# Fused beacon attention and squared-ReLU MLP: attention pairs released at 4.0 per MLP chunk instead of 4.4

## The chip, the cores and the metric

The kernel runs on one core of a Trainium2 chip. The core has a matrix engine (TensorE, PE in the profile, with its weight loads shown apart as PEld), a vector engine (VectorE, DVE), a scalar engine (ScalarE, ACT), a general engine (GpSimd, POOL), and SyncE (SP), which here only issues DMAs. Each engine runs its own instructions in order; the engines meet through semaphores. The metric is the device time of one execution in microseconds (us), lower being better.

## The reference

Inputs are `q`, `k`, `v` of shape 8 x 8 x 576 x 64 (batch, head, position, width), 16 "beacon" keys and values per batch and head, and the two MLP weights. Attention comes first, and its output, laid out as 4608 tokens of 512 numbers, is the input of the MLP:

```python
k_all = np.concatenate([beacon_k, k], axis=2)          # 16 + 576 keys
v_all = np.concatenate([beacon_v, v], axis=2)
scores = scale * np.matmul(q, k_all.transpose(0, 1, 3, 2))
scores = np.where(causal, -1000000000.0, scores)       # beacons are always seen
a = softmax(scores)
attn_out = np.matmul(a, v_all)
x = attn_out.transpose(0, 2, 1, 3).reshape(4608, 512)
h = x @ w_in                                           # 512 -> 2048
out = np.maximum(h, 0.0) ** 2 @ w_out                  # 2048 -> 512
```

All arrays are float32 outside the kernel; on the chip the matrix products take bfloat16 and accumulate in float32.

## The kernel before, in words

**Tiles.** Attention is worked in *pairs*: two heads of one batch. There are 4 pairs in a batch and 32 in all; pair `p` belongs to batch `p // 4`. For one pair the scores (L753, keys as weights, 64 rows per head, the two heads side by side) are cut into four pieces, each in two banks of PSUM, the accumulators of TensorE, which has eight banks. From batch 2 on the 16 pieces of a batch are placed in six groups, called strips here, of 3, 3, 3, 3, 2 and 2 pieces, and a strip goes under the gate of its first pair. ACT takes the exponential of a piece (L768) into a probability tile, DVE masks it (L783, L787), TensorE multiplies it by the values (L803, 30 matmuls a pair, with a column of ones for the sum), and DVE normalizes the result into `xn` (L818, L819).

**From attention to MLP.** For batch 0 TensorE transposes `xn`. For batches 1 to 7 SyncE issues five DMA transposes (L850), one for each tile of tokens, from `xn` into `xT`, once all four pairs of the batch are normalized. `xT` is a ring of 2304 tokens, four batches.

**The MLP** runs over nine chunks of 512 tokens. In the first half of a chunk (L931) each of 16 groups of four matmuls fills one PSUM bank, which ACT (L948) or DVE (L950) empties with the ReLU, and DVE squares two such results at once (L957). In the second half (L968) 64 matmuls accumulate four banks, ACT copies them out (L437), and SyncE stores them (L991). The second half uses a bank for 16 matmuls, the first one for four. Each matmul has a weight load of its own: a chunk has 64 on L931 and 64 on L968. Chunk 0 is split in two column ranges, and chunk 4 wraps around the ring, so that both have 128 shorter matmuls on L931. A chunk covers 512 tokens and a batch 576, so chunk `j` (1 to 7) reads `xT` of batch `j - 1` or before, and of batch `j` only the first tiles: four for chunks 1 and 2, three for chunks 3 and 4, two for 5 and 6, one for 7. Chunk 8 reads the rest of batch 7.

**Loads.** For batches 0 to 2 TensorE transposes queries and keys. For batches 3 to 7 SyncE loads them in float32 to staging buffers (L484, L483; eight buffers), POOL casts them to bfloat16 (L439), and SyncE issues two large DMA transposes per batch (L516), one for the queries and one for the keys. Batch buffers are double: batch `b` reuses those of `b - 2`.

**What sets the order.** A planner in the kernel (`Order.run`, L155) writes down the order of the instructions of each engine when the program is built, by playing the kernel through with modelled durations. Whenever an engine comes free there, it takes the operation of the lowest priority number whose inputs are modelled as ready, whose PSUM banks are free, and whose *gate* is open. On TensorE attention has lower numbers than the MLP, so without gates it would always come first. The gate of a pair (`gate`, L717) opens when the MLP work placed so far on TensorE (`progress`, in modelled us) reaches a value that grows with the pair's number; the first four pairs have none:

```python
return o.progress >= mlp_chunk_us * (LEAD + PACE * (p - HP))
```

`mlp_chunk_us` is 27.7, `LEAD` is -0.4, and `HP` is 4. An operation that would be ready but for its gate is kept as `fallback` (L237 to L246) and taken all the same if the engine has nothing else to do in the model. The chip then runs each engine's list in that order, waiting where something is later than the model had it.

Of the kernel before, what the change touches and what calls it, by code (L numbers as in the profile page):

```python
# [310 lines left out]
def kernel(  # L311
# [395 lines left out]
        return SPLIT if b < NSPLIT else WHOLE  # L707

    mlp_chunk_us = 27.7
    LEAD, PACE = -0.4, 0.225  # L710
    norm_ops = {}

    def add_pair(b, pr):
# [375 lines left out]
```

## Time and profile before

| | us |
|---|---|
| median of 3 runs | 343.65 (343.54 to 343.87) |
| profiled execution | 344.22 |
| its span, first to last instruction | 342.40 |
| TensorE busy | 325.1 |
| ACT busy | 195.0 |
| DVE busy | 160.3 |
| POOL busy | 81.1 |

The profile's page gives busy time by engine, the span in 40 slices, the DMA queues, the chain of work that ended last, and the costliest groups of instructions. Answers of the trace give more: what an engine waited for; the busy time in chosen stretches of the span, also of one line's instructions alone; and the instructions in order of time, where one row is a run of like instructions with its start, its length, what it writes and reads, its count (x) and, in brackets, the idle time before it with what ended that. `L753` is line 753 of the kernel. `SPq` is SyncE's queue, in which a DMA counts from when it is taken up to when it is issued, not to its landing. A group of words such as `kT<-qk_area` names the tile written and the one read.

### The profile page before, as it was taken

How to read it: one execution, taken by the hardware profiler on the slowest of the kernel's cores; microseconds unless marked ns; L12 is line 12 of the kernel's file. 1: busy time of each engine (PE TensorE's matmuls, PEld its weight loads, DVE VectorE, ACT ScalarE, POOL GpSimd, SP SyncE). 2: the span in 40 equal slices, each digit the busy share in tenths (PEclk: the TensorE clock that was granted, in tenths of full speed). 3: DMA queues.
4: the chain of work that ended last, by engine and by line, in shares of the span. 5: the costliest groups of instructions: out<-in, count | busy, mean ns of one | idle time of the engine just before them, and what ended most of it. 6: DMA issues, size and time to landing. Idle time of an engine off the chain costs nothing.

```text
span 342.4 us, 7074 instructions
## 1 busy us (share of the span) xinstructions
PE 325.1 (95%) x2838; PEld 175.7 (51%) x2876; DVE 160.3 (47%) x323; ACT 195.0 (57%) x301; POOL 81.1 (24%) x129
## 2 busy tenths in 40 slices
PE   2999999999999999999999799999999999999995
PEld 2677665454544544453557574444544444444442
DVE  6788978177425842385524483287403202301400
ACT  3987873588358564577554754597326326515611
POOL 6545802516124222423241126020000000000000
PEclk9999999999999999999999999999999999999999
DMA  9999999699979996999999889980041011011002
GB/s 166 197 205 221 206 204 208 134 252 204 188 164 215 197 199 145 255 188 224 133 209 220 184 177 207 219 170 24 15 117 63 0 61 63 0 61 63 0 29 93
DMA packets 139472, 50.33 MB, mean 147 GB/s; under 512 B 125808, under 2 KB 134512, under 8 KB 139440
## 3 DMA queue, kind: packets, MB, share of 16 engines
q1 hardware_dynamic: 129856, 40.91, 58.1%
q0 software_dynamic: 9376, 8.69, 15.5%
q8 instruction: 22, 0.36, 0.5%
q10 hardware_dynamic: 208, 0.29, 0.3%
q14 instruction: 10, 0.08, 0.1%
HBM read 37.22 MB, written 9.44 MB: 136 GB/s over the span
## 4 chain that ended last, share of the span: by engine, by line
PE 66%; DMA 19%; SPq 7%; DVE 4%; issue 2%; POOL 2%; ACT 1%; POOLq 0%; DVEq 0%; ACTq 0%
PE ps L931 28%; PE ps L968 26%; PE ps L803 5%; SPq L850 5%; PE ps L753 5%; DMA kT<-qk_area 5%; DMA stg<-in_k_dram 4%; DMA bks<-in_beacon_k_dram 3%; DMA stg<-in_v_dram 3%; DVE g L957 2%; DMA stg<-in_q_dram 1%; DMA qk_area<-in_q_dram 1%; SPq L484 1%; POOL w_in L892 1%; PE ps L635 1%
## 5 line engine op out<-in xcount | busy, mean ns | idle before, releaser
L931 PE MATMUL ps<-xT,w_in 128*128 128x512 bf16 (+3 forms) x688 | 134.3, 340 | 1.1 <-DMA xT<-xn 0.2
L968 PE MATMUL ps<-w_out,g 128*128 128x512 bf16 x554 | 127.9, 379 | 1.1 <-issue 0.2
L768 ACT ACTIVATE pt<-ps 128x832 bf16<-128x832 f32 (+4 forms) x128 | 102.9, 872 | 28.6 <-PE ps L753 28.5
L931 PEld LDWEIGHTS <-w_in 128*128 128x128 bf16 x704 | 64.9, 98 | 57.8 <-issue 7.7
L957 DVE TENSOR_TENSOR g<-g 128x1024 bf16<-128x1024 bf16 (+2 forms) x80 | 53.6, 673 | 76.9 <-ACT g L948 75.6
L948 ACT ACTIVATE g<-ps 128x512 bf16<-128x512 f32 (+2 forms) x117 | 66.3, 567 | 39.9 <-PE ps L931 39.2
L968 PEld LDWEIGHTS <-g 128*128 128x128 bf16 x576 | 54.1, 98 | 64.1 <-issue 2.9
L437 ACT COPY osb<-ps 128x512 f32<-128x512 f32 x36 | 21.3, 591 | 65.0 <-PE ps L968 60.4
L439 POOL CAST vb<-stg 128x512 bf16<-128x512 f32 (+1 forms) x36 | 24.3, 684 | 84.3 <-DMA stg<-in_v_dram 39.9
L439 POOL CAST qk_area<-stg 128x512 bf16<-128x512 f32 (+2 forms) x50 | 32.1, 645 | 50.6 <-DMA stg<-in_q_dram 33.8
L783 DVE TENSOR_TENSOR pt<-pt,tri 128x1024 bf16<-128x1024 bf16 (+1 forms) x36 | 23.9, 667 | 31.3 <-ACT pt L768 31.3
L803 PEld LDWEIGHTS <-pt 128*128 128x128 bf16 (+1 forms) x960 | 33.6, 98 | 7.6 <-issue 1.2
L950 DVE TENSOR_SCALAR g<-ps 128x512 bf16<-128x512 f32 (+2 forms) x43 | 25.7, 600 | 24.9 <-PE ps L931 24.5
L803 PE MATMUL ps<-vb,pt 128*128 128x65 bf16 (+1 forms) x960 | 34.9, 194 | 1.3 <-DVE pt L783 0.5
L753 PE MATMUL ps<-qT,kT 64*128 64x80 bf16 (+7 forms) x400 | 33.5, 282 | 2.6 <-DMA kT<-qk_area 2.1
L819 DVE TENSOR_TENSOR xn<-ps,rcp 128x640 bf16<-128x640 f32 (+2 forms) x36 | 27.0, 750 | 1.5 <-DVE rcp L818 0.2
L753 PEld LDWEIGHTS <-kT 64*128 64x128 bf16 x400 | 13.5, 96 | 23.2 <-issue 15.4
L818 DVE RECIPROCAL rcp<-ps 128x10 f32<-128x10 f32 (+2 forms) x36 | 7.5, 208 | 23.1 <-PE ps L803 23.0
L437 ACT COPY qT<-ps 128x576 bf16<-128x576 bf16 x12 | 7.5, 640 | 6.4 <-PE ps L635 5.0
L439 DVE COPY kT<-ps 128x576 bf16<-128x576 bf16 x12 | 8.9, 751 | 2.8 <-PE ps L638 1.9
L787 DVE TENSOR_TENSOR pt<-pt,tri 80x160 bf16<-80x160 bf16 x32 | 10.0, 312 | 0.0
L635 PE MATMUL ps<-ident,sparek 96*128 96x96 bf16 x18 | 1.5, 229 | 6.0 <-DVE sparek L439 6.0
(49 smaller groups left out, 71.7 us busy)
## 6 DMA issues: line engine op xcount, KB each, us to landing
out_dram<-osb SPq DMA_DIRECT2D x17, 512.0 KB, 3.3
stg<-in_v_dram SPq DMA_DIRECT2D x21, 256.0 KB, 5.0
stg<-in_q_dram SPq DMA_DIRECT2D x20, 256.0 KB, 4.7
stg<-in_k_dram SPq DMA_DIRECT2D x15, 256.0 KB, 5.1
w_in<-in_moe_w_in_dram POOLq DMA_DIRECT2D x4, 512.0 KB, 8.2
w_out<-in_moe_w_out_dram POOLq DMA_DIRECT2D x4, 512.0 KB, 10.9
stg<-in_v_dram SPq DMA_DIRECT2D x7, 224.0 KB, 4.2
qk_area<-in_k_dram POOLq DMA_DIRECT2D x4, 288.0 KB, 12.7
```

Of the source, the lines that this page charges most:

```text
L437: nc.scalar.copy(dst, src)
L439: eng[e].tensor_copy(dst, src)
L753: nc.tensor.matmul(st[:, hj, col:col + t1 - t0], kT[x.b % 2][hp, x.pr, 128 * c:128 * c + 128], qT[x.b % 2][hp, x.pr, t0:t1], start=True, s ...
L768: nc.scalar.activation(pt[x.take_pt.held[0]][:, :, off:off + width], pair(box["qk"], k)[:, :, 0:width], AF.Exp, bias=0.0, scale=scale)
L783: nc.vector.tensor_tensor(out=d, in0=d, in1=tri[:, m0:m0 + m, :][:, None].to_broadcast([128, 2, m, 128]), op=ALU.min)
L803: nc.tensor.matmul(a[:, hj, (t - tl[0]) * (D + 1):(t - tl[0] + 1) * (D + 1)], P[0:rr, hj, o:o + 128], vb[b % 2][0:rr, c, h, :], start=(c = ...
L819: nc.vector.tensor_tensor(out=xn[b % 2].rearrange("p t (h d) -> p h t d", d=D)[:, 2 * pr:2 * pr + 2, tl[0]:tl[0] + nt], in0=a[:, :, :, 0:D ...
L931: nc.tensor.matmul(h[:, lo - spans[0][0]:hi - spans[0][0]], w_in_sb[:, mc, ft * 128:(ft + 1) * 128], xT[:, mc, lo % RING:lo % RING + hi - lo],
L948: nc.scalar.activation(dst, h, AF.Relu, bias=0.0, scale=1.0)
L950: nc.vector.tensor_scalar(out=dst, in0=h, scalar1=0.0, scalar2=None, op0=ALU.max)
L957: nc.vector.tensor_tensor(out=d, in0=d, in1=d, op=ALU.mult)
L968: nc.tensor.matmul(o, G[:, fc, ts * 128:(ts + 1) * 128], w_out_sb[:, fc, :], start=(fc == 0), stop=(fc == NFT - 1))
```

## The change

`PACE` goes from 0.225 to 0.25. The gates of the 28 gated pairs (4 to 31) run from -0.4 to 5.675 chunks before and from -0.4 to 6.35 after: the last pair is released 0.675 chunk later, and the first at the same place. The last pair of batch `b` is released at `b - 0.65` chunks after the change; before it was at `0.9 b - 0.625`. Nothing else in the kernel is edited; the planner's order follows from the gates.

```diff
     mlp_chunk_us = 27.7
-    LEAD, PACE = -0.4, 0.225
+    LEAD, PACE = -0.4, 0.25
     norm_ops = {}
```

## The prediction

> **What bounds the kernel now.** I read the page's engine rows and clock first, then the list of what TensorE waited for, then the busy time by stretch, and last the order of TensorE and of the SyncE queue around the waits.
>
> ```profile
> PE 325.1 (95%) x2838; PEld 175.7 (51%) x2876; DVE 160.3 (47%) x323; ACT 195.0 (57%) x301; POOL 81.1 (24%) x129
> ...
> PEclk9999999999999999999999999999999999999999
> ```
>
> ```profile
> PE ps L635 <- DVE sparek L439: 6.0, 1, 6.0
> PE ps L753 <- DMA kT<-qk_area: 2.1, 1, 2.1
> PE ps L803 <- DVE xn L819: 0.5, 1, 0.5
> ```
>
> The columns of the second list are us in total, times, longest. TensorE (PE) is the bound: busy 95% of the 342.4 us at full granted clock. Its largest wait, 6.0 us, is the start, before anything that the change touches. The next is one wait of 2.1 us for the transposed keys.
>
> ```profile
> 92.12:253.38 161.26, 157.36 (x1435) 84.32 (x1456) 77.58 (x135) 96.10 (x140) 40.95 (x63) 1.00 0.90 172
> 156.07:190.31 34.24, 32.01 (x305) 18.44 (x308) 14.41 (x26) 20.41 (x30) 10.35 (x16) 1.00 1.12 197
> 253.38:282.75 29.37, 29.21 (x134) 13.32 (x136) 5.53 (x8) 11.89 (x20) 0.00 (x0) 1.00 0.14 54
> ```
>
> A row gives the stretch, its length, busy PE, PEld, DVE, ACT, POOL, the clock and the DMA share. 92.12 to 253.38 holds the attention of batches 3 to 7; TensorE idles there for 161.26 − 157.36 = 3.90 us, 2.23 of it in batch 5's stretch (second row). The third row is MLP alone: 136 weight loads in 29.37 us, 0.216 us each, so a chunk of 128 loads is 27.65 us. ACT (96.10 of 161.26 us) and DVE (77.58) have room. So whatever the order, TensorE's work is the same, and an edit to the order can win at most some part of those 3.90 us.
>
> **Does the gate set the order now?** A pair's scores may be placed once the MLP work already placed reaches the gate. I count that work in chunks, by weight loads of the two MLP lines, cut at the first score strip of batches 3 to 7 and at the last of batches 3, 4, 5 and 7. L931 first, then L968:
>
> ```profile
> 0.00:92.12 92.12, 16.82 (x192) 1.00 1.07 199
> 92.12:113.77 21.65, 1.79 (x20) 1.00 0.92 198
> 113.77:123.84 10.07, 3.77 (x40) 1.00 1.19 200
> 123.84:149.26 25.42, 2.03 (x24) 1.00 0.96 198
> 149.26:156.07 6.81, 2.20 (x24) 1.00 1.14 167
> 156.07:176.99 20.92, 1.79 (x20) 1.00 1.13 185
> 176.99:190.31 13.32, 5.41 (x56) 1.00 1.10 216
> 190.31:220.71 30.40, 7.04 (x76) 1.00 0.99 193
> 220.71:239.06 18.35, 5.32 (x60) 1.00 0.52 112
> ```
>
> ```profile
> 0.00:92.12 92.12, 7.18 (x80) 1.00 1.07 199
> 92.12:113.77 21.65, 4.38 (x48) 1.00 0.92 198
> 123.84:149.26 25.42, 5.97 (x64) 1.00 0.96 198
> 156.07:176.99 20.92, 4.30 (x48) 1.00 1.13 185
> 176.99:190.31 13.32, 1.48 (x16) 1.00 1.10 216
> 190.31:220.71 30.40, 5.89 (x64) 1.00 0.99 193
> ```
>
> Chunks 0 and 4 are split in two column ranges, so their 128 L931 loads count as 64: 64 off the first row, 28 off the x56, 36 off the x76. The sum at 92.12 us is 192 − 64 + 80 = 208, or 1.625 chunks; then 2.156, 2.469, 3.156, 3.344, 3.875, 4.219, 5.031, 5.500. The gates of the first pairs of batches 3 to 7 (pairs 12, 16, 20, 24, 28) are 27.7·(−0.4 + 0.225·(p − 4)) us, in chunks 1.40, 2.30, 3.20, 4.10, 5.00, and the strips came at 1.625, 2.469, 3.344, 4.219, 5.031: behind the gate by 0.23, 0.17, 0.14, 0.12 and 0.03. So batches 3 to 6 started when their keys and queries were expected, and only batch 7 at its gate. After the change the gates are 1.60, 2.60, 3.60, 4.60, 5.60. Batch 3's start stays (1.625 is past 1.60), as does all before it; the orders part about 100 us in, where its third pair's gate rises from 1.85 to 2.10 and that strip now stands at about 2.03. From batch 4 on the gate comes after the data by 0.13, 0.26, 0.38 and 0.57 chunk, and it sets the start.
>
> **Step 1, the wait for the keys goes: −2.07 us.**
>
> ```profile
> 190.32 0.76 PE L753 MATMUL ps<-qT,kT 64*128 64x496 bf16 x8 [2.07 <-DMA kT<-qk_area]
> ```
>
> This is batch 6's first strip: TensorE stood from 188.25 to 190.32 us until the transposed keys landed. With the gate at 4.60 in place of the present 4.219, 0.381·128 = 49 more weight loads stand ahead of it, 49·0.216 = 10.5 us, so TensorE comes there at about 198.8 us at the earliest, 8.5 us after the landing. If that cover is gone (loads later by more than 8.5 us), the wait is back at up to its present size. What releases those keys does not get later by the change: their loads and casts reuse buffers of batch 4, whose last strip moves from 3.156 to about 3.35, some 5 us on from 149 us, and the loads come well behind that. On SyncE's queue the five transposes of attention output (xT) move behind loads that now follow them; loads gain by that, unless an xT stands in the queue before its normalization is done, in which case the loads behind it wait as well, and the 8.5 us have to carry it. What is late next is nothing on TensorE's list: the largest other wait past 92 us is the 0.5 above.
>
> **Step 2, the MLP's input comes later: 0 us, hidden by about 4 us or more.** All pairs of a batch come later, so its normalized output, and the SyncE transposes that make the MLP's input, too. Chunk j reads only the first tiles of batch j: three for chunks 3 and 4, two for chunk 5, one for chunk 7.
>
> ```profile
> 111.43 4.90 SPq L516 DMA_TRANSPOSE qT<-qk_area  x1
> 116.43 3.60 SPq L516 DMA_TRANSPOSE kT<-qk_area  x1
> 120.08 2.52 SPq L484 DMA_DIRECT2D stg<-in_v_dram  x3
> 122.69 6.75 SPq L850 DMA_TRANSPOSE xT<-xn  x5
> 159.49 7.50 SPq L850 DMA_TRANSPOSE xT<-xn  x5
> 189.80 6.72 SPq L850 DMA_TRANSPOSE xT<-xn  x5
> 246.27 6.42 SPq L850 DMA_TRANSPOSE xT<-xn  x5
> ```
>
> ```profile
> DMA to landing us min/median/max: 2.3/2.5/5.7
> ```
>
> ```profile
> 143.23 2.84 PE L931 MATMUL ps<-xT,w_in 128*128 128x512 bf16 x12
> 179.34 1.04 PE L931 MATMUL ps<-xT,w_in 128*128 128x256 bf16 x8
> 217.12 1.03 PE L931 MATMUL ps<-xT,w_in 128*128 128x512 bf16 x4
> 282.98 7.31 PE L931 MATMUL ps<-xT,w_in 128*128 128x512 bf16 x33
> ```
>
> The needed tile of chunk 3 lands at 122.69 + 2·1.35 + 2.5 = 127.9 us, 15.3 us ahead of its first matmul at 143.23. For chunk 4 it is 159.49 + 2·1.50 + 2.5 = 165.0 against 179.34, 14.3 us; for chunk 5, 193.6 against 217.12, 23.5 us; for chunk 7, 248.8 against 282.98, 34.2 us. The last pair of batch b is released at b − 0.65 after the change. The second strips of pairs 15 and 19 now stand 0.08 and 0.18 behind their gates (2.156 against 2.075, 3.156 against 2.975). With 0.08, the shifts are 2.43 − 2.156, 3.43 − 3.156, 4.43 − 3.875 and 6.43 − 5.500 chunks, or 7.6, 7.6, 15.3 and 25.7 us; what stays is 7.7, 6.7, 8.2 and 8.5 us. With 0.18 it is 2.8 less everywhere, at the least 3.9, at chunk 4. I cost it at 0. If the cover goes, each us of lateness beyond it is a us of TensorE, as none of its other work is free to fill it.
>
> **Step 3, small waits in the new order: 0 us, between −1.0 and +2.5.** Of the 3.90 us of idle time, 1.67 lies outside batch 5's stretch: once TensorE waited 0.5 us for DVE in an attention-times-values step (the xn row). MLP alone leaves 29.37 − 29.21 = 0.16 us in 29, or 0.7 in the other 127 us, so the most that the small waits can give is −1.0. The other way, one wait of 0.5 in each of five batches is 2.5 us. Pairs 30 and 31 (gates 6.10 and 6.35) move into chunk 6, where ACT is busy for 11.89 of 29.37 us, so their exponentials find room. The order after 100 us is new, so I take the same number as now, 0 net: the row at hand is one in five batches.
>
> Strips, matmuls, exponentials and DMAs are the same in number, and the last 60 us are MLP alone in both, so steps 1 to 3 are the sum: −2.07 + 0 + 0. The profiled execution took 344.22 us (342.4 span, 1.8 around it), 0.57 above the median of 343.65; after it, 342.15 with a span of 340.3, and the median 343.65 − 2.07 = 341.6 us. The low end is 343.65 − 2.07 − 1.0 = 340.6; the likeliest case's own range ends at 341.6 + 3·0.5 = 343.1, three new small waits.
>
> **The rivals.**
>
> *The wait moves (no change), 0.14.* The supply of batches 4 to 6 was late against the gate throughout, the DMA share in batch 5's stretch is 1.12, and an order that leaves SyncE in another state can have one strip stand ahead of its keys again. Against it: from batch 4 on the gate lies 3.6 to 16 us of MLP work past the present starts. One wait of the same size gives 343.65. That the change does not do what it says belongs here: a gated strip is still placed when TensorE would stand idle in the written order. Pair 23's first strip, for one, stands at 159.54 us, right after batch 5's first and far ahead of its gate of 3.875:
>
> ```profile
> 159.54 0.58 PE L753 MATMUL ps<-qT,kT 64*128 64x496 bf16 x4
> ```
>
> If that took most of them, the time would stay at 343.65.
>
> *The MLP's input is late (slower), 0.17.* At batch 3 the query and key transposes (4.90 + 3.60) and three loads (2.52) stood directly ahead of the xT transposes, 11.1 us of SyncE's queue. If after the change they come between the normalization and the xT of batch 4, chunk 4's input is 11.1 − 6.7 = 4.4 us late, and the time is 341.6 + 4.4 = 346.0 us. It decides from 6.7 + 2.07 = 8.8 us of such lateness. Against it: the xT moves later, away from the transposes of keys, which end at 120.0 us while batch 3's xT would come at about 130.
>
> [...] After the 6.05 us at the start, the first transposes ran slower than the same ones later (per row of six):
>
> ```profile
> 6.05 0.66 PE L635 MATMUL ps<-ident,sparek 96*128 96x96 bf16 x6 [6.05 <-DVE sparek L439]
> 55.28 0.42 PE L635 MATMUL ps<-ident,sparek 96*128 96x96 bf16 x6
> ```
>
> The clock row reads 9 there all the same. [...]
>
> *Many small waits, 0.05.* After the change the last strips of every batch fall in the first half of a chunk, in which every matmul group needs a bank emptied by ACT or DVE; now only batches 3 and 4 have that pattern, with one wait of 0.5 between them. At two waits of 0.5 in each of five batches, 5.0 us, the time is 341.6 + 5.0 = 346.6; it decides from five.
>
> **How the numbers follow.** The forecast, 341.6 us, has 0.64. A measurement here can tell about 0.2%, 0.7 us, from no change. Of the 0.64, 0.61 is faster by more than that and 0.03 within it; of "the wait moves", 0.03 is faster, 0.09 the same and 0.02 slower; the two slower rivals add 0.22 less 0.01. So faster 0.64, same 0.13, slower 0.23. The range goes from 340.6 to 344.5, into the slower rivals' milder forms.
>
> **What would show it.** Step 1: no wait for kT on TensorE past 92 us, and first strips of batches 4 to 7 at 2.6, 3.6, 4.6 and 5.6 chunks. Step 2: no wait of L931 for xT past 92 us, with 4 us or more between landing and first use. Step 3: TensorE's idle time from 92 us to the start of chunk 6 near 1.8 us. It would be wrong if L931 waits at the heads of chunks 3 to 7, or if L753 waits for another batch's keys.

## The result and the profile after

The changed kernel takes 341.27 us (median of 20 runs) against 343.68 us for the kernel before (20 runs); the ratio is 0.9946, with a 95% interval of 0.9923 to 0.9969. The ratio is estimated from the executions that were not in a slower state, and is not the quotient of the two medians, which is 0.9930. The forecast was 341.6 us. The profiled execution took 341.50 us with a span of 339.80.

The page's engine row of the changed kernel, and the list of all that TensorE waited for from 93 us to 340 us (us in total, times, longest):

```profile
PE 324.1 (95%) x2838; PEld 175.5 (52%) x2876; DVE 161.4 (47%) x324; ACT 194.5 (57%) x300; POOL 82.3 (24%) x129
```

```profile
PE ps L968 <- issue: 0.6, 4, 0.2
```

The 2.1 us for the keys (L753 <- kT) are gone, and so is the 0.5 us for DVE. What is left is four times 0.16 us.

The stretches of the changed kernel between the first score strips of batches 3, 4, 5, 6 and 7, all engines (columns as in the prediction), and after them a stretch of the same length as the prediction's 161.26 us:

```profile
92.93:128.34 35.41, 35.14 (x292) 17.27 (x296) 16.80 (x29) 20.92 (x31) 11.81 (x18) 1.00 1.03 200
128.34:163.74 35.40, 35.02 (x292) 17.29 (x296) 17.31 (x29) 21.02 (x31) 11.43 (x17) 1.00 1.10 200
163.74:199.32 35.58, 35.31 (x358) 23.54 (x360) 17.84 (x28) 21.62 (x32) 12.65 (x18) 1.00 0.96 200
199.32:234.73 35.41, 35.03 (x292) 17.27 (x296) 16.24 (x29) 21.12 (x31) 6.90 (x11) 1.00 0.78 145
...
92.93:254.19 161.26, 159.71 (x1393) 84.88 (x1414) 73.95 (x126) 96.59 (x143) 42.80 (x63) 1.00 0.88 174
```

Every batch now takes 35.4 to 35.6 us, with 0.27 to 0.38 us of idle time. Over 161.26 us TensorE idles for 1.55 us in place of 3.90.

The weight loads of the MLP in the same stretches, L931 first, then L968:

```profile
0.00:92.93 92.93, 16.79 (x192) 1.00 1.09 199
92.93:128.34 35.41, 5.88 (x64) 1.00 1.03 200
128.34:163.74 35.40, 5.88 (x64) 1.00 1.10 200
163.74:199.32 35.58, 12.13 (x128) 1.00 0.96 200
199.32:234.73 35.41, 5.88 (x64) 1.00 0.78 145
```

```profile
0.00:92.93 92.93, 7.19 (x80) 1.00 1.09 199
92.93:128.34 35.41, 5.87 (x64) 1.00 1.03 200
128.34:163.74 35.40, 5.88 (x64) 1.00 1.10 200
163.74:199.32 35.58, 5.89 (x64) 1.00 0.96 200
199.32:234.73 35.41, 5.86 (x64) 1.00 0.78 145
```

With chunk 4's 128 counted as 64, the stretches hold 128 loads each: exactly one chunk between first strips, which come at 1.625, 2.625, 3.625, 4.625 and 5.625 chunks. From batch 4 on that is 0.025 past the gate, so the gate sets the start.

The gain lies in the part from batch 3's first strip to the last matmul: 246.32 us before (92.12 to 338.44) and 242.96 after (92.93 to 335.89), 3.36 us less. The start before it has the same order in both and was 0.81 us longer in this execution of the changed kernel. Over all profiled executions with batch 3's first strip at 1.625 chunks, that strip came between 92.1 and 94.6 us, so the start varies by more than 2 us whatever the kernel (the last section says where). Below, "the late part" is the time from batch 3's first strip to the end of the last matmul, which leaves that variation out.

### The profile page after: what moved, and what is told of

Its sections match the earlier page's. It is cut to its first block, busy times and chain, and to the rows that moved or that the text cites. A ratio compares the mean times of both kernels' runs of the same rounds, so it can differ in the third digit from the quotient of the medians.

```text
span 339.8 us, 7073 instructions
## 1 busy us (share of the span) xinstructions
PE 324.1 (95%) x2838; PEld 175.5 (52%) x2876; DVE 161.4 (47%) x324; ACT 194.5 (57%) x300; POOL 82.3 (24%) x129
## 4 chain that ended last, share of the span: by engine, by line
PE 86%; DMA 6%; DVE 3%; issue 2%; ACT 1%; POOL 1%; SPq 0%; DVEq 0%; ACTq 0%; POOLq 0%
PE ps L968 36%; PE ps L931 34%; PE ps L803 8%; PE ps L753 7%; DMA bks<-in_beacon_k_dram 3%; DMA qk_area<-in_q_dram 1%; DMA stg<-in_v_dram 1%; DVE qk_area L439 1%; DVE g L957 1%; PE ps L635 1%; POOL w_in L892 0%; DVE g L950 0%; DVE pt L783 0%; ACT qT L437 0%; ACT pt L768 0%
## 5 line engine op out<-in xcount | busy, mean ns | idle before, releaser
L931 PE MATMUL ps<-xT,w_in 128*128 128x512 bf16 (+3 forms) x689 | 134.1, 340 | 1.5 <-DMA w_in<-in_moe_w_in_dram 0.7
L968 PE MATMUL ps<-w_out,g 128*128 128x512 bf16 x553 | 128.3, 379 | 1.5 <-issue 0.6
L768 ACT ACTIVATE pt<-ps 128x832 bf16<-128x832 f32 (+4 forms) x128 | 102.9, 873 | 24.5 <-PE ps L753 24.3
L931 PEld LDWEIGHTS <-w_in 128*128 128x128 bf16 x704 | 64.9, 98 | 56.3 <-issue 4.9
L968 PEld LDWEIGHTS <-g 128*128 128x128 bf16 x576 | 53.8, 98 | 64.6 <-issue 4.6
L957 DVE TENSOR_TENSOR g<-g 128x1024 bf16<-128x1024 bf16 (+2 forms) x80 | 52.3, 658 | 67.7 <-ACT g L948 67.1
L439 POOL CAST vb<-stg 128x512 bf16<-128x512 f32 (+1 forms) x36 | 25.2, 708 | 75.6 <-DMA stg<-in_v_dram 61.3
L803 PEld LDWEIGHTS <-pt 128*128 128x128 bf16 (+1 forms) x960 | 33.7, 97 | 6.6 <-DVE pt L783 0.5
L803 PE MATMUL ps<-vb,pt 128*128 128x65 bf16 (+1 forms) x960 | 35.1, 194 | 0.3 <-ACT pt L768 0.2
L753 PE MATMUL ps<-qT,kT 64*128 64x80 bf16 (+7 forms) x400 | 33.6, 282 | 0.4 <-ACT pt L768 0.4
L753 PEld LDWEIGHTS <-kT 64*128 64x128 bf16 x400 | 13.6, 96 | 21.9 <-issue 17.3
```

The costliest lines, as they stand in the source:

```text
L439: eng[e].tensor_copy(dst, src)
L753: nc.tensor.matmul(st[:, hj, col:col + t1 - t0], kT[x.b % 2][hp, x.pr, 128 * c:128 * c + 128], qT[x.b % 2][hp, x.pr, t0:t1], start=True, s ...
L768: nc.scalar.activation(pt[x.take_pt.held[0]][:, :, off:off + width], pair(box["qk"], k)[:, :, 0:width], AF.Exp, bias=0.0, scale=scale)
L803: nc.tensor.matmul(a[:, hj, (t - tl[0]) * (D + 1):(t - tl[0] + 1) * (D + 1)], P[0:rr, hj, o:o + 128], vb[b % 2][0:rr, c, h, :], start=(c = ...
L931: nc.tensor.matmul(h[:, lo - spans[0][0]:hi - spans[0][0]], w_in_sb[:, mc, ft * 128:(ft + 1) * 128], xT[:, mc, lo % RING:lo % RING + hi - lo],
L957: nc.vector.tensor_tensor(out=d, in0=d, in1=d, op=ALU.mult)
```

## The experiments

All times are medians, and ratios are to the kernel before, measured beside the experiment.

**1. Only the wait taken away.** The order of every engine stays that of the kernel before.

```diff
-                    st = pair(box["qk"], k)
+                    st, kept = pair(box["qk"], k), (x.b + (group[0][0].p == 24 and group[0][1] == 0)) % 2
...
-                                kT[x.b % 2][hp, x.pr, 128 * c:128 * c + 128],
-                                qT[x.b % 2][hp, x.pr, t0:t1],
+                                kT[kept][hp, x.pr, 128 * c:128 * c + 128],
+                                qT[kept][hp, x.pr, t0:t1],
```

> Every engine keeps the order of the kernel before; only the first score strip of batch 6 reads the keys and queries of batch 5, which lie ready, in place of its own (that strip's scores are therefore another batch's). Theory A (the gain is the wait of batch 6's first strip for its keys): the wait of 2.07 us at L753 goes and nothing takes its place, 343.7 - 2.1 = 341.6 us, ratio about 0.994. Rival B (the gain is the even spacing of the strips, and the wait alone would be paid later): the time stays within 0.7 us of 343.7, since the strips stand as close as before.

Measured: 343.01 us, ratio 0.9967 (0.9939 to 0.9995); late part 245.09 us, 1.23 less than before. TensorE's order of time around three places (start, length, what, count, and in brackets the wait):

```profile
189.93 0.76 PE L753 MATMUL ps<-qT,kT 64*128 64x496 bf16 x8
...
201.19 0.66 PE L803 MATMUL ps<-vb,pt 80*128 80x65 bf16 x16 [1.04 <-POOL vb L439]
...
221.94 0.76 PE L753 MATMUL ps<-qT,kT 64*128 64x496 bf16 x8 [0.35 <-DMA kT<-qk_area]
```

The first strip of batch 6 runs without a wait, but 1.39 us come back further on: TensorE, now earlier, meets batch 6's values before POOL has cast them, and batch 7's keys before they land. The interval of the ratio reaches from theory A's 0.994 almost to 1, so the run times do not decide between A and B; the trace does. Of the 1.23 us, 0.47 is the wait for DVE (L803 for `xn`, at 112.8 us in the kernel before), which is absent here although the order there is the same. So taking the 2.07 us away won some 0.8 us and not 2.07, and what is missing came back as new waits: theory A was too simple. The wait is real, and it is the first of several that all say the same: in batches 6 and 7 the supply on the chip runs behind the written order. I call this theory A2: the change gains because it puts *all* of those uses behind the supply.

**2. Half of the change.** `PACE` 0.2375.

```diff
-    LEAD, PACE = -0.4, 0.225
+    LEAD, PACE = -0.4, 0.2375
```

> PACE 0.2375, half of the change. Batch 6's first strip is placed at 4.37 chunks in place of 4.21, 0.16*27.65 = 4.4 us later, more than the wait of 2.07 us. Theory A: no wait for the keys of batch 6, and nearly the whole gain, 341.6 us. Rival B: half of the spread gives about half of the gain, 342.6 us, or less.

Measured: 341.46 us, ratio 0.9931 (0.9907 to 0.9956); late part 243.17 us; no wait over 0.2 us after 92 us. Half of the spread has the whole gain, against rival B.

**3. Batch 6 alone later.**

```diff
-            return o.progress >= mlp_chunk_us * (LEAD + PACE * (p - HP))
+            return o.progress >= mlp_chunk_us * (LEAD + (0.25 if b == 6 else PACE) * (p - HP))
```

> The kernel before, with the gates of batch 6's four pairs alone at PACE 0.25: its first strip moves from 4.21 to 4.62 chunks, the order is the same up to there, and batch 7's strips are pressed together with those of batch 6 (the last one at 5.81). Theory A: the wait goes and the time is 341.6 us. Rival B: the strips stand closer together than in either kernel, so small waits take the gain away, 343 to 344 us.

Measured: 342.66 us, ratio 0.9964 (0.9940 to 0.9988); late part 244.75 us, 1.57 less than before. What TensorE waited for after 92 us:

```profile
PE ps L753 <- DMA kT<-qk_area: 1.1, 1, 1.1
PE ps L968 <- issue: 0.3, 2, 0.2
PE ps L803 <- DVE xn L819: 0.2, 1, 0.2
```

The wait for keys is now batch 7's (at 220.7 us), whose first strip was moved from 5.03 to 5.21 chunks only. Neither number was met: about half of the gain, and most of what is missing is again the supply (1.1 us) and not closer strips.

**4. The lead without the pace.** Every gate 0.2 chunk later at the old pace.

```diff
-    LEAD, PACE = -0.4, 0.225
+    LEAD, PACE = -0.2, 0.225
```

> PACE 0.225 as before, but LEAD -0.2 in place of -0.4: every gate 0.2 chunk later, batch 6's first strip at 4.34 chunks (0.13*27.65 = 3.6 us later than before) and batch 7's at 5.21. Theory A2: no wait for batch 6's keys, most of the gain, 341.6 us, without any change of pace. Rival B: within 0.7 us of the time before, 343.5 us.

Measured: 341.27 us, ratio 0.9949 (0.9929 to 0.9970); late part 243.21 us; no wait at all listed after 93 us. The gain is had with pairs at 4.4 per chunk.

**5. The pace without the lead.** The new pace, with every gate 0.4 chunk earlier.

```diff
-    LEAD, PACE = -0.4, 0.225
+    LEAD, PACE = -0.8, 0.25
```

> PACE 0.25 as after the change, but LEAD -0.8 in place of -0.4: every gate 0.4 chunk earlier, so that batches 3 to 6 are placed where they stand in the kernel before (batch 6's first strip at 4.21), and batch 7 at 5.21. Theory A2: the wait for batch 6's keys is back, 1 to 2 us, and the time is 343 to 343.7 us although pairs are released at four per chunk. Rival B (the pace, the even spacing, brings the gain): 341.5 us.

Measured: 343.14 us, ratio 0.9996 (0.9963 to 1.0030); late part 245.50 us, 0.82 less than before. Batch 6's first strip in TensorE's order of time:

```profile
189.81 0.76 PE L753 MATMUL ps<-qT,kT 64*128 64x496 bf16 x8 [2.00 <-DMA kT<-qk_area]
```

The wait is back at its old size, and the gain in run time is gone although pairs are released at four per chunk. Of the 0.82 us in the late part, 0.47 is the wait for DVE that does not show here, and 0.07 the keys'. Experiments 4 and 5 together settle it: the pace by itself is worth nothing that the run time shows, and some 0.3 us in the late part; where the strips of batches 6 and 7 stand against their supply is what counts.

**6. No late supply at all.** Batches 6 and 7 read the buffers of the batch before, with the matmul lines of experiment 1.

```diff
+                    st, kept = pair(box["qk"], k), (x.b + (x.b >= 6)) % 2
...
-                            vb[b % 2][0:rr, c, h, :],
+                            vb[(b + (b >= 6)) % 2][0:rr, c, h, :],
```

> The order of the kernel before on every engine, but batches 6 and 7 read the keys, queries and values of the batch before them, which lie ready (their attention is therefore of the wrong batch). With the first strip alone on old keys, 1.39 us of new waits came: values of batch 6 (1.04), keys of batch 7 (0.35). Theory A2 (the chip's supply runs behind the written order in batches 6 and 7, and the change's gain is the cover against that): no wait on kT or vb past 180 us, 341.6 us, a ratio near 0.994, and near 244.2 us from batch 3's first strip to the last matmul (246.3 before, 243.0 after the change). Rival B2 (the even order itself saves more than 1 us): about 342.5 us or more, near 245 us in that part.

Measured: 354.65 us, ratio 1.0344 (1.0307 to 1.0381). TensorE's waits after 92 us:

```profile
PE ps L803 <- POOL vb L439: 3.0, 1, 3.0
PE ps L753 <- DMA kT<-qk_area: 2.8, 1, 2.8
```

The edit did not do what it was meant to: waits on values and keys grew instead of going. The last key transpose on SyncE's queue, and batch 6's last strip on TensorE, show why:

```profile
212.47 2.97 SPq L516 DMA_TRANSPOSE kT<-qk_area  x1
```

```profile
219.11 1.16 PE L753 MATMUL ps<-qT,kT 64*128 64x464 bf16 x10 [2.81 <-DMA kT<-qk_area]
```

That transpose is batch 7's, and it landed 6.60 us after its issue, at 219.07. It fills the buffer that batch 6 now reads, and in the written order it stands ahead of this strip, so the strip waited for batch 7's keys. In the same way the wait of 3.01 us ended with a cast of batch 7's values. On top came the clock, which fell to 0.50 after each of the two waits (last section). So the late uses of batch 6 were tied to a later supply, and the run tells nothing on A2.

**7. The change taken twice.** `PACE` 0.275.

```diff
-    LEAD, PACE = -0.4, 0.225
+    LEAD, PACE = -0.4, 0.275
```

> PACE 0.275, the change taken twice. Last strips of batches 3, 6 and 7 are placed at 2.75, 5.93 and 6.80 chunks (after the change 2.44, 5.43 and 6.43). With the change the MLP input of chunks 3, 6 and 7 lands 5.1, 10.0 and 6.3 us ahead of its first use; 8.6, 13.8 and 10.2 us later it would be late by 3.5, 3.8 and 3.9 us, so the theory that each us of lateness past the cover is a us of TensorE gives 341.3 + 11 = 352 us, with waits of L931 for xT of this size. Rival: batch 7 and batch 3 are filled with other work in the written order, and the time stays under 345 us.

Measured: 354.79 us, ratio 1.0325 (1.0286 to 1.0364). The two largest entries of TensorE's waits after 92 us:

```profile
PE ps L753 <- ACT pt L768: 4.4, 6, 1.3
PE ps L931 <- DMA xT<-xn: 2.6, 2, 1.8
```

That the time is near the expectation is luck, as its make-up is another: the waits for xT are smaller than 11 us, and a larger part stands at the strips. At the heads of chunks 3 and 6 the written order has strips placed one after the other, some ahead of their gates (at chunk 3 both strips of batch 4's last pair, whose gate is at 3.725), as nothing else was ready there in the model; on the chip most of them wait for ACT's exponentials to empty their banks. Read so, the late MLP input is paid there more than at L931. On top came the clock. Stretches around the first of these places, and two rows of TensorE's order of time in it:

```profile
139.80:143.60 3.80, 1.19 (x14) 0.58 (x14) 0.18 (x1) 3.80 (x7) 1.84 (x3) 1.00 0.77 157
143.60:150.40 6.80, 5.83 (x47) 3.18 (x45) 2.56 (x7) 2.76 (x4) 0.00 (x0) 0.50 0.71 168
```

```profile
145.04 1.86 PE L931 MATMUL ps<-xT,w_in 128*128 128x512 bf16 x4 [0.75 <-DMA xT<-xn]
146.70 1.86 PE L803 MATMUL ps<-vb,pt 128*128 128x65 bf16 x30
```

The same step in the changed kernel:

```profile
143.52 1.08 PE L803 MATMUL ps<-vb,pt 128*128 128x65 bf16 x30
```

After 3.8 us in which TensorE was busy for 1.19 us only, the granted clock is 0.50 for 6.8 us. Four MLP matmuls take 1.86 us where they took 1.03 us, and the 30 matmuls on the values 1.86 us where they took 1.08. All waits listed after 92 us come to 8.2 us; the 10.2 us at a granted 0.50 (a second place has 3.4) cost some 4.5 us by estimate, at the 0.83 us that the four matmuls lose in 1.86. Together that is 12.7 of the 13.5 us by which this kernel is slower than the changed one.

**8. The new pace, later still.** `LEAD` -0.2 at `PACE` 0.25.

```diff
-    LEAD, PACE = -0.4, 0.225
+    LEAD, PACE = -0.2, 0.25
```

> PACE 0.25 with LEAD -0.2: every gate 0.2 chunk later than after the change, the last strips of batches 3 to 7 at 2.62, 3.56, 4.62, 5.56 and 6.62 chunks against 2.44, 3.43, 4.43, 5.43 and 6.43, so 3.6 to 5.2 us later. After the change the MLP input lands 4.0 to 10 us ahead of its use (least at chunk 4, 4.0, and chunk 3, 5.1). If that cover is what it seems, there is at most 1 us of waits of L931 for xT in all, and the time is 341.3 to 342.5 us. Rival (the cover is thinner than the landing times say): several waits for xT, 344 us or more.

Measured: 345.66 us, ratio 1.0079 (1.0051 to 1.0106): slower than before. TensorE's waits after 92 us, then the last normalization of batch 5 on DVE, SyncE's queue behind it, and TensorE's first matmul of chunk 5:

```profile
PE ps L931 <- DMA xT<-xn: 4.4, 3, 2.5
```

```profile
204.58 0.82 DVE L819 TENSOR_TENSOR xn<-ps,rcp 128x640 bf16<-128x640 f32 x1
```

```profile
204.68 4.92 SPq L516 DMA_TRANSPOSE qT<-qk_area  x1
209.69 3.14 SPq L516 DMA_TRANSPOSE kT<-qk_area  x1
212.92 6.43 SPq L850 DMA_TRANSPOSE xT<-xn  x5
```

```profile
216.72 1.47 PE L931 MATMUL ps<-xT,w_in 128*128 128x512 bf16 x6 [2.46 <-DMA xT<-xn]
```

The rival of this run held. The waits at the heads of chunks 3, 4 and 5 are 1.48, 0.51 and 2.46 us. The landing times behind the expectation were worked out from a median, and for chunk 3 the changed kernel had 3.7 us of cover (see step 2 below) and not 5.1; a shift of 5.2 us is 1.5 us too much, which is the wait. At chunk 5 the cover was 5.4 us, and there the shift changed what stands ahead of xT in SyncE's queue: batch 5's last pair was normalized at 205.4 us, its xT was issued at 212.9, behind the two transposes of queries and keys that hold the queue for 8.1 us.

**9. Between the two limits, and the change once more.** `LEAD` -0.5 at `PACE` 0.25:

```diff
-    LEAD, PACE = -0.4, 0.225
+    LEAD, PACE = -0.5, 0.25
```

> PACE 0.25 with LEAD -0.5: every gate 0.1 chunk earlier than after the change, between the keys on one side (batch 6's first strip at 4.56) and the MLP input on the other (last strips of batches 3 to 7 at 2.34, 3.34, 4.34, 5.33 and 6.33). If the gain is cover against late keys and its limit is cover against late MLP input, both are kept here with 4 us or more: no wait on kT and none on xT past 92 us, 341.3 us, the same as the change within 0.7 us. Rival (the change sits on a best point, and an earlier gate gives part of the gain back): 342 us or more.

Measured: 341.12 us, ratio 0.9930 (0.9903 to 0.9957); late part 243.21 us, and no wait of TensorE listed after 93 us.

> The changed kernel once more, beside the one with LEAD -0.5 on one chip: 341.3 us, ratio 0.994 to 0.995, and no wait on kT or xT past 92 us in a second profiled execution. If the first profile was a lucky one, such a wait of 0.5 us or more shows here.

Measured: 341.37 us, ratio 0.9948 (0.9918 to 0.9978); late part 242.95 us, against 242.96 in the first profile, with the same waits. The changed kernel, `PACE` 0.2375, and the two other leads (-0.2 at 0.225, -0.5 at 0.25) can't be told apart: their ratios lie between 0.9930 and 0.9949, with intervals of about 0.0025 either way. Nothing that was run beats the change clearly.

## Why the prediction was right, by its own steps

**Does the gate set the order?** Right. Batch 3 starts at 1.625 in both, and batches 4 to 7 at 0.025 past the new gates.

**Step 1, the wait for the keys: right in size, too narrow in its mechanism.** The wait went (-2.07). The strip now starts at 199.33 us (198.8 was the earliest forecast). The transposed keys were issued at 185.02 us and landed 7.8 us later, at 192.8, so the cover is 6.5 us, where 8.5 was forecast. The step also said that what releases the keys does not get later. They landed 2.5 us later than before (190.3), of which 0.81 is the start: between batch 6's query and key transposes SyncE's queue now holds eight loads and stores (177.70 to 184.92), where before it held one store. The forecast cover was large enough to carry this. The step said that what would be late next is nothing on TensorE's list. Experiment 1 shows that this holds only because the change moves batch 7, and batch 6's values, as well: with the wait alone taken away, 1.04 and 0.35 us appear elsewhere, and the late part gains 1.23 us, 0.47 of it the wait for DVE, and not 2.07. The list of waits of a profile shows the first of a row of late arrivals and not the ones that its own delay covers.

SyncE's queue, TensorE's strip, and the time from issue to landing, all of the changed kernel:

```profile
185.02 4.62 SPq L516 DMA_TRANSPOSE kT<-qk_area  x1
```

```profile
199.33 0.76 PE L753 MATMUL ps<-qT,kT 64*128 64x496 bf16 x8
```

```profile
DMA to landing us min/median/max: 7.8/7.8/7.8
```

**Step 2, the MLP's input: right at 0, with less cover than forecast.** SyncE's xT runs of batches 3 and 4 and the first matmuls of chunks 3 and 4 in the changed kernel:

```profile
130.85 7.43 SPq L850 DMA_TRANSPOSE xT<-xn  x5
...
167.61 6.76 SPq L850 DMA_TRANSPOSE xT<-xn  x5
```

```profile
141.80 1.89 PE L931 MATMUL ps<-xT,w_in 128*128 128x512 bf16 x8
...
177.21 1.04 PE L931 MATMUL ps<-xT,w_in 128*128 128x256 bf16 x8
```

By the prediction's way of counting, chunk 3's third tile lands at 130.85 + 2·1.49 + 2.5 = 136.3 us, 5.5 ahead of its use (7.7 forecast, 4.9 at the longer lag), and chunk 4's at 172.8, 4.4 ahead (6.7, or 3.9). But 2.5 us from issue to landing is a median. For chunk 3's tile itself the trace has:

```profile
133.93 1.26 SPq L850 DMA_TRANSPOSE xT<-xn  x1
```

```profile
DMA to landing us min/median/max: 4.2/4.2/4.2
```

It landed at 138.1 us, 3.7 ahead of its use, a little under the 4 us that the prediction named as the sign of this step; chunk 4's landed at 173.0, 4.2 ahead. So the cover is real and thin. Experiment 8 shows what it costs to use it up: 0.2 chunk more is enough to be slower than before.

**Step 3, small waits: sized a little short.** It was put at 0 net. The idle time fell from 3.90 to 1.55 us, by 0.28 more than the keys' 2.07; up to the start of chunk 6 it is 1.50, where the step had 1.8. The 0.5 us wait for DVE did not return, but that is not the new order's merit alone: with the old order at that place it was 0.47 us in the kernel before, 0.23 in experiment 3, and absent in experiments 1 and 6. The late part fell by 3.36 us; 2.35 of it is idle time, and the remaining 1.0 us is in rows counted as busy and is not resolved further. Beside the keys' 2.07 the late part thus gained 1.29 us, a little past the step's low end of -1.0. In the median the gain is 343.68 - 341.27 = 2.4 us, 0.3 more than the sum; by the ratio it is 1.9 us, 0.2 less. That the median came within 0.3 us of the forecast is in part luck, since the start alone varies by more than that from execution to execution.

**The rivals.** "The wait moves" is what happens when only the wait is removed (experiment 1) or only batch 6 is moved (experiment 3), and what was forecast did not need. "The MLP's input is late" is the one that bounds this change: its mechanism, transposes of queries and keys ahead of xT, stood in experiment 8 as described, at chunk 5 and not at chunk 4. "Many small waits" was not seen: strips in the first half of a chunk cost no wait in the changed kernel.

The clock was no part of the change: in the changed kernel it is 1.00 throughout the late part. In experiments 6 and 7 it fell to 0.50: in experiment 6 after single waits of 3.01 and 2.81 us, and in experiment 7, where the longest single wait at these places was 1.29 us, after 1.19 us of work in 3.8 us. That the prediction's clock row reads 9 at the start, where six transposes took 0.66 us and later 0.42 us, has a plain reason: the trace of the kernel before has no record of the clock until 12.75 us, and without one the view prints full clock.

## What to carry to other kernels

When an order is written out ahead by a model and the chip's supply lags behind it, look for the first wait of the bounding engine on a transfer, and give all uses after it some microseconds of cover, not that one alone; a shift of the whole schedule does as well as a new pace. Then look at the other end: what the shift makes late, and above all what stands ahead of it in the same queue, since that decides how far one can go. Here the usable stretch was narrow: with the first strip of batch 6 at 4.21 chunks 2 us were lost to late keys, between 4.34 and 4.62 nothing, and at 4.81 more than 4 us to late MLP input.

## What the runs showed of the hardware that I had not expected

In experiments 6 and 7 the granted clock fell to 0.50. In experiment 7 TensorE had waits of at most 1.29 us at the two places, but was busy only 1.19 of 3.80 us, and the granted clock was then 0.50 for 6.8 us; the second place had 1.15 us of work in 3.7 us, and 3.4 us at 0.50. Experiment 6, around its wait of 3.01 us (columns as in the prediction):

```profile
208.85:212.27 3.42, 0.41 (x15) 0.40 (x14) 0.00 (x0) 0.59 (x1) 1.84 (x3) 1.00 1.29 216
212.27:215.68 3.41, 3.41 (x29) 1.79 (x25) 1.05 (x2) 0.00 (x0) 0.61 (x1) 0.50 1.15 225
```

After its wait of 2.81 us the clock was 0.50 again, from 219.09 to 222.51 us. In experiment 8 a single wait of 2.46 us, with 3.54 us of work in the 6 us around it, left the clock at 1.00, and so did the 2.07 us in the kernel before. So the clock was 0.50 here after single waits of 3.01 and 2.81 us and stayed at 1.00 after one of 2.46 us, and it was 0.50 as well after several shorter ones close together (at most 1.29 us); what decides it, these runs do not show.

The time up to batch 3's first strip, with the same order, was between 92.1 and 94.6 us in the profiled executions. The record of the clock begins between 12.4 and 24.3 us, depending on the execution. In the kernel before, where it begins at 12.75 us, four score matmuls of one shape took 0.35 us at 15.30 us already. In experiment 1, where it begins at 24.26 us, four of this shape took 0.53 us at 19.35 and 0.35 us at 25.36:

```profile
19.35 0.53 PE L753 MATMUL ps<-qT,kT 64*128 64x336 bf16 x4
...
25.36 0.35 PE L753 MATMUL ps<-qT,kT 64*128 64x336 bf16 x4
```

The two executions that came to batch 3 last, at 94.5 (`LEAD` -0.5) and 94.6 us (experiment 1), are the two whose record begins last, at 24.1 and 24.3 us; their first MLP matmul comes at 21.2 us, against 18.5 to 20.6 in the others. That slower matmuls at the start make part of the difference is my estimate from these rows; what the clock was there, no record shows.

The late part of the changed kernel came out at 242.96 and 242.95 us in its two profiles. For edits that act there it is a finer measure than the run time, but two profiles of one kernel are few, and with one order the wait for DVE alone differed by 0.47 us.
